# Attention and squared-ReLU layers on one core: one more batch of the first product by seven block products, with the sums moved to fit

## The chip, the cores and the metric

One core of a Trainium2 chip. The time is the device time of the kernel in microseconds (us). The kernel before takes 370.7 us: a median of 370.71 in three runs (370.69 to 371.02).

## The reference, cut to what matters

```python
# q, k, v: (8 batches, 12 heads, 448 rows, 64), fp32;  w_in: (768, 2048);  w_out: (2048, 768)
scores = (q @ k.T) / 8
attn_out = (maximum(scores, 0) ** 2 / 448) @ v        # per batch and head
x = attn_out as (8 * 448, 768)
h = x @ w_in
g = maximum(h, 0) ** 2
out = g @ w_out                                       # (3584, 768), fp32
```

## The kernel before

The kernel works in fp16 with sums in fp32. TensorE is kept busy with one long stream: h of batch 0, h of batch 1, the first O stage (`out` for the batches 0 and 1), h of batch 2, h of batch 3, the second O stage, and so on. The attention of later batches is spliced into this stream as "visits": two score tiles each time (8 matmuls), and, when a unit of four heads has all its tiles, its product with v (28 matmuls). ScalarE takes each score tile out of PSUM (where the matmuls leave their sums) with a Relu, VectorE squares it in SBUF (where the operands lie), and the product with v waits for that square.

h is made in two ways. For the batches 0 and 1 it is made directly:

```python
def h_group(b, f):                       # 16 groups f of 128 columns of w_in
    ...
        nc.tensor.matmul(cell[0][:, 0:S],                    # 6 matmuls of 448 columns
            lhsT=w1[f // 4][:, m, (f % 4) * P:(f % 4 + 1) * P],
            rhs=xts[b][:, m, :], start=(m == 0), stop=(m == NM - 1))
        ...                              # then Relu (ScalarE or VectorE), square (VectorE)
```

For the batches 2 to 7 it is made by a Strassen-like scheme: seven products of half-size blocks in place of eight. Each half of the work (`i0` 0 and 4) is 14 products of six 224-column matmuls. The scheme costs sums elsewhere: eight of w_in once (`sums_w1`), four of x for each batch (`sums_x`), and sums of products as they come out of PSUM:

```python
order = (                                # (group, product, PSUM bank, fresh bank, what follows)
    (0, 1, 0, True,  lambda: copy(0, 0, "m1", "a")),         # ScalarE: PSUM to SBUF
    (1, 1, 0, True,  lambda: copy(1, 0, "m1", "b")),
    (0, 2, 1, True,  lambda: plus(0, 1, "m1", False, False)),# VectorE: PSUM + copy, Relu, to g
    (0, 6, 0, False, lambda: copy(0, 0, "u2", "c")),         # adds into the bank just copied
    ...
    (0, 4, 0, False, lambda: relu21(0)),                     # ScalarE: Relu to g, then a square
    (1, 4, 0, False, lambda: relu21(1)),
    (0, 3, 1, False, lambda: c12(0)),                        # VectorE: sum to g, then a square
    (1, 3, 1, False, lambda: c12(1)))
```

The O stages always use such a scheme, with eight sums of w_out (`sums_w2`) made once. Before, all eight `sums_w2` and six of the eight `sums_w1` are made by VectorE during the direct h of batch 1, and the other two during the first O stage. A simple model in the kernel (`at_pe`, `at_ve`) keeps track of how far TensorE and VectorE are, and puts squares that can wait where VectorE should be free. It has no clock for ScalarE.

Of the kernel before, what the change touches and what calls it, by code (L numbers as in the profile page):

```python
# [18 lines left out]
def kernel(  # L19
# [45 lines left out]
    at_p = ctx.enter_context(tc.tile_pool(name="atp", bufs=10))  # L65
    x_p = ctx.enter_context(tc.tile_pool(name="xp", bufs=3))
    g_p = ctx.enter_context(tc.tile_pool(name="gp", bufs=1))
    early = ExitStack()
    q16_p = early.enter_context(tc.tile_pool(name="q16p", bufs=3))

# [268 lines left out]

    due: deque = deque()  # L340
    due_g: deque = deque()
    at_pe = [0.0]
    at_ve = [0.0]

# [8 lines left out]
        fn()  # L353

    def fill(until):
        for d in (due, due_g):
            while d and max(at_ve[0], at_pe[0], d[0][0]) + d[0][1] <= until:
                put(d)

# [38 lines left out]
            gts[b // 2] = g_p.tile([P, NF, 2 * S], FP16, name="g", tag="g")  # L398
        return gts[b // 2]

    def h_group(b, f):
        z = (b % 2) * S
        cell = [None]

        def step(m):
            def run():
                if m == 0:
                    cell[0] = mm_tile()
                nc.tensor.matmul(  # L409
                    cell[0][:, 0:S],  # L410
                    lhsT=w1[f // 4][:, m, (f % 4) * P:(f % 4 + 1) * P],
                    rhs=xts[b][:, m, :], start=(m == 0), stop=(m == NM - 1))
                if m < NM - 1:
                    return
                f0 = f - f % 2
                g = g_of(b)[:, f0:f0 + 2, z:z + S]
                if b == 0 and (f % 2 == 1 or f == 0) and f < 14:
                    nc.vector.tensor_scalar(
                        out=g[:, f % 2], in0=cell[0][:, 0:S],
                        scalar1=0.0, scalar2=None, op0=ALU.max)  # L420
                else:
                    nc.scalar.activation(
                        out=g[:, f % 2], in_=cell[0][:, 0:S], func=AF.Relu)
                flush()
                if b == 0 and f == NF - 1:
                    square(g)
                elif f % 2 == 1:
                    nc.vector.tensor_mul(g, g, g)
            return run

        return [(0.1892, step(m), m == 0) for m in range(NM)]
# [26 lines left out]
    def h_period(b, i0, extra):  # L458

        z = (b % 2) * S  # L460
        XY = [[None, None], [None, None]]
        keep: dict = {}

        def gs(s, hi, right=None):
            f = i0 + 2 * s + (8 if hi else 0)
            c = (slice(z, z + S) if right is None
                 else slice(z + Q, z + S) if right else slice(z, z + Q))
            return g_of(b)[:, f:f + 2, c]

        def acc(s, y):  # L470
            return XY[s][y][:, 0:S].rearrange("p (r c) -> p r c", r=2)

        def copy(s, y, nm, tag):
            t = late["m"].tile([P, S], FP32, name=nm, tag=tag)
            nc.scalar.activation(out=t, in_=XY[s][y][:, 0:S], func=AF.Copy)
            keep[s, nm] = t.rearrange("p (r c) -> p r c", r=2)

        def plus(s, y, nm, hi, right):

            now_ve(0.54)  # L480
            nc.vector._custom_dve(  # L481
                TENSOR_ADD_SAT, out=gs(s, hi, right), in0=acc(s, y),
                in1=keep[s, nm], s0=3.4e38, s1=0.0)

        def rest(g, lag):
            due_g.append((at_pe[0] + lag, 0.54,
                          lambda: nc.vector.tensor_mul(g, g, g), b))

        def relu21(s):
            nc.scalar.activation(out=gs(s, True, False), in_=acc(s, 0), func=AF.Relu)  # L490
            rest(gs(s, True), 0.8)

        def c12(s):
            plus(s, 1, "u2", False, True)
            rest(gs(s, False), 0.0)

        def left(k, f, m):

            c, n = f // 4, slice((f % 4) * P, (f % 4 + 1) * P)
            if k in (1, 2):  # L500
                return w1[c][:, m + NH * (k - 1), n]
            if k in (4, 7):
                return w1[c + 2][:, m + (NH if k == 4 else 0), n]
            return wsum[{5: 0, 6: 1, 3: 2}[k], c][:, m, n]

        def right(k, m):
            if k in (1, 2):
                return xts[b][:, m + NH * (k - 1), 0:Q]
            if k in (3, 7):
                return xts[b][:, m + (NH if k == 3 else 0), Q:S]  # L510
            return xsum[b, {5: 0, 6: 1, 4: 3}[k]][:, m]


        order = (
            (0, 1, 0, True, lambda: copy(0, 0, "m1", "a")),
            (1, 1, 0, True, lambda: copy(1, 0, "m1", "b")),
            (0, 2, 1, True, lambda: plus(0, 1, "m1", False, False)),
            (0, 6, 0, False, lambda: copy(0, 0, "u2", "c")),
            (1, 6, 0, False, lambda: copy(1, 0, "u2", "d")),
            (1, 2, 1, True, lambda: plus(1, 1, "m1", False, False)),  # L520
            (0, 5, 1, True, lambda: copy(0, 1, "m5", "a")),
            (0, 7, 0, False, lambda: plus(0, 0, "m5", True, True)),
            (1, 7, 0, False, lambda: copy(1, 0, "u3", "b")),
            (1, 5, 1, True, lambda: plus(1, 1, "u3", True, True)),
            (0, 4, 0, False, lambda: relu21(0)),
            (1, 4, 0, False, lambda: relu21(1)),
            (0, 3, 1, False, lambda: c12(0)),
            (1, 3, 1, False, lambda: c12(1)))

        FREE = {2: 0.6, 5: 0.6, 7: 0.1, 9: 0.6, 12: 0.6, 13: 1.0, 16: 0.6}  # L530

        def step(p, r, m):
            s, k, y, fresh, end = order[p]

            def run():
                if fresh and r == 0 and m == 0 and k != 5:
                    XY[s][y] = mm_tile(s)
                nc.tensor.matmul(  # L538
                    XY[s][y][:, r * Q:(r + 1) * Q],
                    lhsT=left(k, i0 + 2 * s + r, m), rhs=right(k, m),  # L540
                    start=(fresh and r == 0 and m == 0), stop=(m == NH - 1),
                    skip_group_check=not (fresh and r == 0))
                if r == 1 and m == NH - 1:
                    end()
                    for fn in extra.get(p, ()):
                        fn()
                    nx = min(n for n in FREE if n > p)
                    fill(at_pe[0] + (nx - p) * 0.576 + 0.25 + FREE[nx])
            return run



        return [(0.096, step(p, r, m), r == 0 and m == 0 and p not in (0, 1, 6, 8))
                for p in range(14) for r in range(2) for m in range(NH)]
# [8 lines left out]
                    "(p j) d -> p j d", j=J)[:, j, c],  # L563
                in_=osb[64 * i:64 * i + 64, c])

    late: dict = {}
    saved: dict = {}

    def tile_of(row):
# [289 lines left out]



    f0, f1 = h_group(0, 0), h_group(0, 1)

    def some(part):
        for _, fn, _ in part:
# [15 lines left out]
    T_H = NF * T_G  # L881
    T_S = 28 * 6 * 0.096
    T_O = [(4 if pr % 2 else 3) * 7 * KH * 0.1625 for pr in range(B // 2)]
    begin = [sum(T_O[:pr]) + 2 * (T_H + T_S * (pr - 1)) * (pr > 0) for pr in range(B // 2)]

    events = []
    seq = [[2, 3], 4, [4, 5], [6, 7], [8, 9], 5, [10, 11], [12, 13], [14, 15],
# [7 lines left out]

    def ready():
        early.close()
        for nm, n in (("s", 1), ("m", 1), ("osb", 2), ("g6", 1), ("ws", 1), ("xs", 1)):
            late[nm] = ctx.enter_context(
                tc.tile_pool(name=nm + "late", bufs=n, reuse_waits="tile"))  # L900

    events.append((T_H + 0.2, ready))
    for i in range(8):
        events.append((T_H + (1 + i // 2) * T_G, lambda i=i: sums_w2(i)))
    for i in range(6):
        events.append((T_H + (8 + i) * T_G, lambda i=i: sums_w1(i)))
    for i in range(2):
        events.append((2 * T_H + 6 + 8 * i, lambda i=i: sums_w1(6 + i)))
    for m in (6, 7):
        events.append((T_H + (1 + 3 * (m - 6)) * T_G, lambda m=m: prefetch(m)))  # L910
    at0 = T_H + 8 * T_G
    for pr in range(1, B // 2):
        t0 = 2 * NB0 * pr
        end = begin[pr] + T_S - 6.5
# [13 lines left out]
        return run  # L928

    periods: dict = {}  # L930
    for b in range(2, B):
        for i0 in (0, 4):
            extra: dict = {}
            if i0 and b % 2 == 0:
                for p, i in ((9, 0), (9, 1), (13, 2), (13, 3)):
                    extra.setdefault(p, []).append(
                        lambda b=b, i=i: sums_x(b + 1, i))
            if i0 and b % 2 == 1:
                extra[9] = [pre(b // 2, 1)]
                extra[13] = [pre(b // 2, 2)]  # L940
            periods[b, i0] = h_period(b, i0, extra)
    outs = [o_steps(pr) for pr in range(B // 2)]
    for i in (1, 2):
        events.append((2 * T_H - (3 - i) * T_G, lambda i=i: outs[0][1](i)))

    steps = [(0.1892, None, False)] * 10 + f1[4:6]
    for f in range(2, NF):
        steps += h_group(0, f)
    for f in range(NF):
        steps += h_group(1, f)  # L950
    steps += outs[0][0]
    for pr in range(1, B // 2):
        for b in (2 * pr, 2 * pr + 1):
# [6 lines left out]
    for cost, fn, edge in steps:  # L960
        fired = 0
        while ev and edge and ev[0][0] <= clock + (1.6 if edge == 2 and not fired else 1e-3):
            if len(ev[0]) == 3:
                if clock < last + 1.5:
                    break
                last = clock
            ev.popleft()[1]()
# [36 lines left out]
```

## Time and profile before

| | before |
|---|---|
| median of 3 runs | 370.71 us |
| span of the profiled run | 368.9 us, clock 0.998 |
| TensorE busy | 359.6 us (97%) |
| VectorE, ScalarE busy | 265.4 us (72%), 247.5 us (67%) |

A busy share averages stages with different limits, so the chain of work that ended last and the single stretches must be read with it. TensorE's rows in the timeline overlap (a 448-column row lasts 0.35 us, the next begins 0.19 us after it): what a stream costs is read from start to start. The view of TensorE's waits before is short; outside the first 24 us, no wait is longer than 0.3 us:

```profile
PE slot L262 <- ACT at L266: 1.4, 6, 0.3
PE mm L725 <- DVE s L594: 0.2, 1, 0.2
PE slot L317 <- DVE at L369: 0.2, 1, 0.2
```

(Who waited, for whom: us in total, number of times, the longest. "slot" at L262 are scores, at L317 the attention product with v, "mm" the products of h and `out`.)

### The profile page before, as it was taken

What the parts mean: (1) busy time and instruction counts of PE and PEld (TensorE: products, weight loads), DVE (VectorE), ACT (ScalarE), POOL (GpSimd) and SP (SyncE); (2) the same over time, 40 slices, a digit from 0 to 9 for tenths busy, and PEclk for the clock granted to TensorE, in tenths of its full rate; (3) what the DMA queues carried; (4) which work ended last, traced back from release to release, by engine and by line L of the source; (5) the groups of instructions that cost most, each with busy time, mean ns of one, the idle gap of its engine ahead of it and who ended that gap; (6) DMA issues with size and microseconds to landing.
All of it is one profiled execution on the core that took longest, in us unless ns stands there. A gap on an engine that the chain in (4) does not pass through costs nothing.

```text
span 368.9 us, 8720 instructions
## 1 busy us (share of the span) xinstructions
PE 359.6 (97%) x3588; PEld 230.3 (62%) x3588; DVE 265.4 (72%) x470; ACT 247.5 (67%) x371; POOL 107.1 (29%) x128
## 2 busy tenths in 40 slices
PE   8899999999999999999999999999999999999994
PEld 3644445445555778875555588786555689976663
DVE  2997677997777787788585766989766686884442
ACT  3988894787676989876556588886765885532220
POOL 8545521846553155531225045140000000000001
PEclk9999999999999999999999999999999999999999
DMA  8999999999999999967699899692323300003333
GB/s 115 191 207 203 205 204 162 161 158 165 190 166 127 184 101 98 115 93 62 140 166 105 159 155 86 88 116 37 65 71 88 85 3 2 2 0 85 87 92 81
DMA packets 121159, 42.64 MB, mean 116 GB/s; under 512 B 100832, under 2 KB 117760, under 8 KB 121120
## 3 DMA queue, kind: packets, MB, share of 16 engines
q0 software_dynamic: 82912, 23.01, 62.3%
q1 hardware_dynamic: 38048, 18.98, 25.7%
q8 instruction: 28, 0.46, 0.5%
q10 hardware_dynamic: 160, 0.10, 0.1%
q14 instruction: 11, 0.09, 0.1%
HBM read 45.61 MB, written 11.01 MB: 153 GB/s over the span
## 4 chain that ended last, share of the span: by engine, by line
PE 90%; ACT 3%; DVE 3%; issue 2%; DMA 1%; POOL 0%; POOLq 0%; ACTq 0%
PE mm L725 34%; PE mm L538 27%; PE slot L262 10%; PE mm L409 9%; PE slot L317 7%; ACT at L266 3%; DMA k<-in_k_dram 1%; DVE at L297 1%; PE avt L280 1%; PE slot L238 1%; PE mm L238 0%; DVE at L369 0%; DVE xt L292 0%; ACT u L627 0%; DVE osb L632 0%
## 5 line engine op out<-in xcount | busy, mean ns | idle before, releaser
L266 ACT ACTIVATE at<-slot 128x896 f16<-128x896 f32 x168 | 145.8, 925 | 22.2 <-PE slot L262 22.2
L369 DVE TENSOR_TENSOR at<-at 128x896 f16<-128x896 f16 x147 | 87.1, 617 | 9.7 <-ACT at L266 9.6
L109 POOL DMA_DIRECT2D qs<-in_q_dram x36 | 35.3, 983 | 113.7 <-DMA qT<-qs 106.2
L725 PEld LDWEIGHTS <-s 128*128 128x128 f16 x440 | 41.5, 98 | 32.7 <-issue 3.6
L262 PE MATMUL slot<-qT,kT 64*64 64x448 f16 x744 | 56.8, 361 | 1.9 <-ACT at L266 1.4
L538 PEld LDWEIGHTS <-w 128*128 128x128 f16 x576 | 54.3, 98 | 5.1 <-issue 4.3
L538 PE MATMUL mm<-xt,w 128*128 128x224 f16 x432 | 48.9, 259 | 0.0
L725 PEld LDWEIGHTS <-g 128*128 128x128 f16 x336 | 31.7, 98 | 24.1 <-issue 4.7
L538 PEld LDWEIGHTS <-ws 128*128 128x128 f16 x432 | 40.3, 98 | 4.7 <-issue 4.7
L632 DVE SCALAR_TENSOR_TENSOR osb<-mm,u 128x384 f32<-128x384 f32 (+1 forms) x30 | 16.2, 542 | 36.4 <-ACT u L627 24.0
L725 PE MATMUL mm<-b,g 128*128 128x384 f16 x224 | 40.7, 326 | 0.0
L725 PE MATMUL mm<-b,s 128*128 128x384 f16 x216 | 39.6, 326 | 0.2 <-DVE s L594 0.2
L409 PE MATMUL mm<-xt,w 128*128 128x448 f16 x192 | 39.8, 354 | 0.0
L725 PE MATMUL mm<-t,s 128*128 128x384 f16 x224 | 39.3, 326 | 0.0
L109 POOL DMA_DIRECT2D ks<-in_k_dram x36 | 35.1, 976 | 9.4 <-DMA b<-in_moe_w_out_dram 5.8
L262 PEld LDWEIGHTS <-kT 64*64 64x64 f16 x744 | 19.0, 104 | 28.7 <-issue 23.3
L561 POOL DMA_DIRECT2D out_dram<-osb x2 | 1.1, 563 | 119.6 <-DVE osb L632 119.6
L627 ACT ACTIVATE u<-mm 128x384 f32<-128x384 f32 x28 | 13.8, 492 | 31.6 <-PE mm L725 27.1
L538 PE MATMUL mm<-x,ws 128*128 128x224 f16 x288 | 34.1, 259 | 0.0
L481 DVE CUSTOM_DVE_ANT_0 g<-mm,m 128x448 f16<-128x448 f32 x36 | 22.4, 622 | 15.1 <-PE mm L538 7.3
L317 PE MATMUL slot<-at,vt 64*64 64x448 f16 x588 | 31.9, 350 | 0.2 <-DVE at L369 0.2
L409 PEld LDWEIGHTS <-w 128*128 128x128 f16 x192 | 17.1, 98 | 19.2 <-issue 5.1
(76 smaller groups left out, 399.7 us busy)
## 6 DMA issues: line engine op xcount, KB each, us to landing
out_dram<-osb SPq DMA_DIRECT2D x52, 192.0 KB, 3.0
vt<-in_v_dram POOLq DMA_DIRECT2D x24, 224.0 KB, 6.2
qs<-in_q_dram POOLq DMA_DIRECT2D x36, 112.0 KB, 4.6
ks<-in_k_dram POOLq DMA_DIRECT2D x36, 112.0 KB, 5.0
w<-in_moe_w_in_dram POOLq DMA_DIRECT2D x8, 384.0 KB, 11.9
b<-in_moe_w_out_dram POOLq DMA_DIRECT2D x4, 768.0 KB, 17.1
q<-in_q_dram POOLq DMA_DIRECT2D x6, 224.0 KB, 7.9
k<-in_k_dram POOLq DMA_DIRECT2D x6, 224.0 KB, 8.3
```

Source lines behind the costliest of these rows:

```text
L109: nc.gpsimd.dma_start(out=t[:, :, hh, :], in_=heads(src, n)[:, hh].rearrange("p (j d) -> p j d", d=D))
L238: nc.tensor.transpose(pss[i][64 * hh:64 * hh + 64, i if n < 4 else 0, j * P:(j + 1) * P], src[:, hh, j * D:(j + 1) * D], ident)
L262: nc.tensor.matmul(ps[c, hh, 0:S], lhsT=kT[r, j, c], rhs=qT[r, :, c], start=True, stop=True)
L266: nc.scalar.activation(out=at, in_=ps[:, :, 0:S], func=AF.Relu, scale=SK)
L317: nc.tensor.matmul(ps[64 * hh:64 * hh + 64, hp, 0:S], lhsT=vt[r, hh, j * D:(j + 1) * D], rhs=at[r, hh, :], start=(j == 0), stop=(j == J - 1))
L369: lambda: nc.vector.tensor_mul(at, at, at), 0))
L409: nc.tensor.matmul(cell[0][:, 0:S], lhsT=w1[f // 4][:, m, (f % 4) * P:(f % 4 + 1) * P], rhs=xts[b][:, m, :], start=(m == 0), stop=(m == NM ...
L481: nc.vector._custom_dve(TENSOR_ADD_SAT, out=gs(s, hi, right), in0=acc(s, y), in1=keep[s, nm], s0=3.4e38, s1=0.0)
L538: nc.tensor.matmul(XY[s][y][:, r * Q:(r + 1) * Q], lhsT=left(k, i0 + 2 * s + r, m), rhs=right(k, m), start=(fresh and r == 0 and m == 0), ...
L627: nc.scalar.activation(out=t, in_=X[0][:, 0:HALF], func=AF.Copy, scale=CO)
L632: nc.vector.scalar_tensor_tensor(out=osb[row][:, c], in0=acc[0][:, 0:cc.stop - cc.start], scalar=CO, in1=keep[nm][:, cc], op0=ALU.mult, op ...
L725: nc.tensor.matmul(acc[0][:, 0:HALF], lhsT=left()[:, f], rhs=right[:, f], start=(fresh and f == 0), stop=(f == KH - 1), skip_group_check=n ...
```

## The change

h of batch 1 is made by the block products too. For that the sums of w_in must be there earlier: six of the eight go into h of batch 0, two into h of batch 1. The sums of w_out are fitted between the products of h of batch 1, six of its eight squares of g move from VectorE to ScalarE, and the visits of batch 2 begin later and follow each other more closely. The core of the diff (pools, names and unused branches are cut):

```diff
-        def rest(g, lag):
+        def square_g(g, later, lag):
+            if not later:
+                nc.scalar.activation(out=g, in_=g, func=AF.Square)
+                return
             due_g.append((at_pe[0] + lag, 0.54,
                           lambda: nc.vector.tensor_mul(g, g, g), b))
         def relu21(s):
-            rest(gs(s, True), 0.8)
+            square_g(gs(s, True), b > 1, 0.8)
         def c12(s):
-            rest(gs(s, False), 0.0)
+            square_g(gs(s, False), b > 1 or i0, 0.0)
 ...
-    for i in range(8):
-        events.append((T_H + (1 + i // 2) * T_G, lambda i=i: sums_w2(i)))
     for i in range(6):
-        events.append((T_H + (8 + i) * T_G, lambda i=i: sums_w1(i)))
+        events.append(((5, 7, 8, 10, 11, 13)[i] * T_G,
+                       lambda i=i: sums_w1((0, 2, 4, 1, 3, 5)[i])))
+    events.append((15 * T_G, lambda: sums_x(1, 0)))
+    events.append((T_H, lambda: sums_w1(6)))
+    for i in (0, 1, 4, 5, 2, 3, 6, 7):
+        due_w.append((27.5 if i > 5 else 24.0, 0.87, lambda i=i: sums_w2(i), 0))
+    for t, left in ((-4.5, 6), (-2.5, 4), (0.0, 2), (1.3, 0)):
+        events.append((T_1 + t, lambda left=left: some_w(left)))
-    at0 = T_H + 8 * T_G
+    at0 = T_H + 0.75 * T_S
 ...
-    for f in range(NF):
-        steps += h_group(1, f)
+    for i0 in (0, 4):
+        steps += periods[1, i0]
 ...
-                if clock < last + 1.5:
+                if clock < last + 1.25:
```

More of the change, by code (lines that the diff above doesn't have):

```diff
@@ L67 @@
     g_p = ctx.enter_context(tc.tile_pool(name="gp", bufs=1))
+    late = {nm: ctx.enter_context(tc.tile_pool(name=nm + "late", bufs=1, side="right"))
+            for nm in ("ws", "xs", "m")}
     early = ExitStack()
@@ L341 @@
     due_g: deque = deque()
+    due_w: deque = deque()
     at_pe = [0.0]
@@ L355, in fill @@
     def fill(until):
-        for d in (due, due_g):
+        for d in (due, due_g, due_w):
             while d and max(at_ve[0], at_pe[0], d[0][0]) + d[0][1] <= until:
@@ L399, in g_of, with h_group @@
         return gts[b // 2]
-    def h_group(b, f):
-        z = (b % 2) * S
+    def h_group(f):
         cell = [None]
@@ L411, in run @@
                     lhsT=w1[f // 4][:, m, (f % 4) * P:(f % 4 + 1) * P],
-                    rhs=xts[b][:, m, :], start=(m == 0), stop=(m == NM - 1))
+                    rhs=xts[0][:, m, :], start=(m == 0), stop=(m == NM - 1))
                 if m < NM - 1:
@@ L415, in run @@
                 f0 = f - f % 2
-                g = g_of(b)[:, f0:f0 + 2, z:z + S]
-                if b == 0 and (f % 2 == 1 or f == 0) and f < 14:
+                g = g_of(0)[:, f0:f0 + 2, 0:S]
+                if (f % 2 == 1 or f == 0) and f < 14:
                     nc.vector.tensor_scalar(
@@ L424, in run @@
                 flush()
-                if b == 0 and f == NF - 1:
+                if f == NF - 1:
                     square(g)
@@ L564, in store @@
                 in_=osb[64 * i:64 * i + 64, c])
-    late: dict = {}
     saved: dict = {}
@@ L858 @@
         name="mma", bufs=2, space=PSUM, reuse_waits="tile")))
-    f0, f1 = h_group(0, 0), h_group(0, 1)
+    f0, f1 = h_group(0), h_group(1)
     def some(part):
@@ L883 @@
     T_O = [(4 if pr % 2 else 3) * 7 * KH * 0.1625 for pr in range(B // 2)]
-    begin = [sum(T_O[:pr]) + 2 * (T_H + T_S * (pr - 1)) * (pr > 0) for pr in range(B // 2)]
+    begin = [sum(T_O[:pr]) + (T_H + T_S * (2 * pr - 1)) * (pr > 0) for pr in range(B // 2)]
+    T_1 = T_H + T_S
     events = []
@@ L897, in ready @@
         early.close()
-        for nm, n in (("s", 1), ("m", 1), ("osb", 2), ("g6", 1), ("ws", 1), ("xs", 1)):
+        for nm, n in (("s", 1), ("osb", 2), ("g6", 1)):
             late[nm] = ctx.enter_context(
@@ L902, with some_w @@
     events.append((T_H + 0.2, ready))
-    for i in range(8):
-        events.append((T_H + (1 + i // 2) * T_G, lambda i=i: sums_w2(i)))
     for i in range(6):
-        events.append((T_H + (8 + i) * T_G, lambda i=i: sums_w1(i)))
-    for i in range(2):
-        events.append((2 * T_H + 6 + 8 * i, lambda i=i: sums_w1(6 + i)))
+        events.append(((5, 7, 8, 10, 11, 13)[i] * T_G,
[4 more added lines that the diff above has]
+        due_w.append((27.5 if i > 5 else 24.0, 0.87, lambda i=i: sums_w2(i), 0))
+    def some_w(left):
+        while len(due_w) > left:
+            put(due_w)
+    for t, left in ((-4.5, 6), (-2.5, 4), (0.0, 2), (1.3, 0)):
+        events.append((T_1 + t, lambda left=left: some_w(left)))
     for m in (6, 7):
         events.append((T_H + (1 + 3 * (m - 6)) * T_G, lambda m=m: prefetch(m)))
-    at0 = T_H + 8 * T_G
+    at0 = T_H + 0.75 * T_S
     for pr in range(1, B // 2):
@@ L930 @@
     periods: dict = {}
-    for b in range(2, B):
+    for b in range(1, B):
         for i0 in (0, 4):
             extra: dict = {}
+            if b == 1 and i0 == 0:
+                for p, i in ((0, 1), (1, 2), (5, 3)):
+                    extra[p] = [lambda i=i: sums_x(1, i)]
+                extra[9] = [lambda: sums_w1(7)]
             if i0 and b % 2 == 0:
@@ L937 @@
                         lambda b=b, i=i: sums_x(b + 1, i))
-            if i0 and b % 2 == 1:
+            if i0 and b % 2 == 1 and b > 1:
                 extra[9] = [pre(b // 2, 1)]
@@ L943 @@
     for i in (1, 2):
-        events.append((2 * T_H - (3 - i) * T_G, lambda i=i: outs[0][1](i)))
+        events.append((T_1 - (3 - i) * 1.15, lambda i=i: outs[0][1](i)))
     steps = [(0.1892, None, False)] * 10 + f1[4:6]
     for f in range(2, NF):
-        steps += h_group(0, f)
-    for f in range(NF):
-        steps += h_group(1, f)
+        steps += h_group(f)
+    for i0 in (0, 4):
+        steps += periods[1, i0]
     steps += outs[0][0]
```

## The prediction

> **What bounds the kernel now.** I read first the busy shares of the engines, then the slices, then the chain that ended last.
>
> ```profile
> span 368.9 us, 8720 instructions
> PE 359.6 (97%) x3588; PEld 230.3 (62%) x3588; DVE 265.4 (72%) x470; ACT 247.5 (67%) x371; POOL 107.1 (29%) x128
> PE   8899999999999999999999999999999999999994
> DVE  2997677997777787788585766989766686884442
> PEclk9999999999999999999999999999999999999999
> PE 90%; ACT 3%; DVE 3%; issue 2%; DMA 1%; POOL 0%; POOLq 0%; ACTq 0%
> ```
>
> TensorE is the bound: full in every slice but the first two and the last, at full clock, and 90% of the chain that ended last is its own matmuls. There is no slack behind it, so a product taken away is worth its whole time, and a new wait of TensorE costs its whole time too. VectorE is at 72% on average, but the average hides the stretch that the change touches. The table of busy time by stretch, for h of batch 0 and then h of batch 1:
>
> ```profile
> 24.00:56.60 32.60, 32.04 (x343) 14.47 (x336) 23.67 (x43) 26.95 (x36) 14.42 (x17) 1.00 1.28 204
> 56.60:78.70 22.10, 22.10 (x146) 10.34 (x146) 20.20 (x29) 15.83 (x26) 10.57 (x12) 1.00 1.85 157
> ```
>
> (Columns: stretch, length, busy PE, PEld, DVE, ACT, POOL.) In the second row TensorE is busy 22.10 of 22.10 us and VectorE already 20.20: it makes the sums of both weights there. In the first, VectorE is busy 23.67 of 32.60 and ScalarE 26.95.
>
> The rates, from the chain in order of time and from the timeline of VectorE:
>
> ```profile
> 56.65 10.32 PE mm L409 x54
> 305.48 21.96 PE mm L538 x228
> 59.05 1.82 DVE L152 TENSOR_TENSOR t<-b,b 128x1536 f16<-128x1536 f16 x2
> 46.63 1.15 DVE L369 TENSOR_TENSOR at<-at 128x896 f16<-128x896 f16 x2
> 49.08 2.66 ACT L266 ACTIVATE at<-slot 128x896 f16<-128x896 f32 x3
> ```
>
> A 448-column matmul costs 10.32/54 = 0.191 us in a stream, a 224-column one 21.96/228 = 0.0963. A single row's duration (0.35 and 0.26) has the pipeline's depth in it and is not used. One VectorE instruction overlaps the next by about 0.07 us: 0.87 us a weight sum, 0.54 a square, 0.54 a sum that reads PSUM, 0.42 a sum of x, 0.60 a sum of g. ScalarE takes some 0.83 us for 896 columns and 0.45 for 448 in a row, and 0.92 and 0.54 until the result is there.
>
> **What the Trainium skill says.** "TensorE: Matmul & The Clock Gate", Part 2, step 3: throughput is one column of the moving operand per cycle, so halving columns halves a matmul. The trace agrees: 0.0963 against 0.191. "VectorE: DVE Perf Modes", the perf-mode tier table: tensor_tensor reaches at most 2x on 16-bit operands in SBUF and 1x with PSUM. The trace agrees: a 128x896 square out of SBUF and a 128x448 sum with PSUM both take 0.62. So nothing on VectorE gets cheaper by being moved. "ScalarE: Activation LUTs", step-by-step: one element per cycle and lane whatever the function, so a Square of 128x896 should cost what a Relu of that size costs, some 0.83 us in a row; that is an estimate, as no ScalarE square is in this trace. It is dearer than the same square on VectorE (0.54).
>
> **The change part by part.**
>
> Removed: 96 matmuls of 448 columns, 96 x 0.191 = 18.35 us. Added: 28 products of 6 matmuls of 224 columns, 168 x 0.0963 = 16.18 us. Gain on the bounding engine **2.17 us**. By the order of the two programs all other matmuls are the same in number, and the streams are broken by scores 86 times in both.
>
> Added to VectorE: 12 sums from PSUM (6.5 us) and four sums of x (1.7), less eight squares of g on 896 columns, of which six go to ScalarE and two stay late (4.3 - 1.1 = 3.2): +5 us, in a stretch two us shorter that had 2 us free. Therefore six of the eight sums of w_in (6 x 0.87 = 5.2 us) move into h of batch 0, and two of them come in from the O stage. ScalarE gets 12 copies and 6 squares for its 16 Relus. All this is beside TensorE only where it is in time. I walked the new orders with the durations above and found three places where it is not.
>
> (a) In h of batch 0 the fourth sum of w_in stands straight ahead of the squares of visit 12, 13. Before, these were made at 46.63 to 47.78, and the attention product that reads the second of them reaches it at about 47.86 (start 46.72, 24 of 28 matmuls at 0.047). With 0.87 us ahead of it the square ends at 48.65: TensorE waits **0.8 us**. The sixth sum is ahead of the squares for the last attention product; 0.47 us of idle time is there to take it and the rest, some **0.3 us**, is waited for (before, TensorE already waited for that square at 56.27). The first, second, third and fifth fall in gaps of 1 to 2 us and cost nothing. Their weights landed: the last was issued at 28.86 and takes 12 us.
>
> (b) Between the two halves of h of batch 1 ScalarE has in a row Relu, Square, Relu, three Squares, and then the copy of the first product of the second half. Call T the start of h of batch 1. Product 11 starts at T + 5.9 and its Relu 0.78 later at T + 6.6 (as in the trace, matmul start to consumer). Then Relu 0.54 + 0.06, Square 0.83, Relu 0.60, three Squares 2.5, copy 0.54: T + 11.7. The fourth product of the second half adds into the bank which that copy reads, and TensorE comes to it at 0.1 + 17 x 0.576 = T + 9.9. It waits about **1.7 us**.
>
> (c) From the eighth product of the second half on, VectorE has without a gap: four sums from PSUM 2.2, seven squares of scores 3.8, two of g 1.1, the last four sums of w_out 3.5, s1 and s2 1.2, one output sum 0.5, so 12.3 us up to the last square for the attention product inside the first O group. TensorE needs about 10.8 us to get there: seven products 4.0, three pairs of scores 1.7, two O products 2.6, another pair 0.6, an O product and half a pair 1.6, most of the attention product. The wait is some **1 to 2 us**; ScalarE, late with its Squares, holds up the scores' buffers and the first O copy in the same place. I put 1.7.
>
> Sum: -2.17 + 0.8 + 0.3 + 1.7 + 1.7 = +2.3 us, which makes 373.0. The visits of batch 2 begin some 3 us later and closer together (one per 1.95 instead of 2.19 us of the schedule's clock); they use gaps that VectorE (28.4 of 40.1 us busy) and ScalarE (28.0) have in the first O stage, and move no total. Transfers stay as they are.
>
> **The rivals.**
>
> *Everything stays hidden.* Then only TensorE's work counts: 370.7 - 2.2 = 368.5. For it: VectorE was already at 20.2 of 22.1 without TensorE losing time, and the change has evidently been fitted by a schedule that tracks VectorE's time. Against it: the edge at 47.8 and the row of ScalarE in (b), which that schedule does not track.
>
> *Half of it.* (a) and part of (b) are real, and (c) is taken up because squares can be made earlier than I put them: stalls of 1.5 to 2.5, 370 to 371.
>
> *VectorE becomes the bound for longer.* If the backlog of (c) is carried through the first O stage with its closer visits, each attention product waits again: 2 us more, 375. Against it: VectorE has 12 us to spare in that stage, even after three more visits.
>
> *Transfers.* Closer visits ask for q, k and v of a unit every 7 us or so instead of 8. Against a wait there: they are asked for two units ahead, the median from issue to landing is about 5 us for a load and 4.3 for a transpose.
>
> **Range and chances.** The walk gives 373.0; the first two rivals together have perhaps two chances in five, because a change so carefully placed was probably tried out. I settle at **372.4 us**. The gain can't be more than 2.17, and the stalls I see add to 4.5 at most about 6.5, so the range is **369.6 to 374.8**. Faster by 2% would need 7.4 us (chance 0.01); slower by 2% the same the other way (0.03); within 2% 0.96.
>
> **What would show it.** In the profile after: the h products of batch 1 as 168 more rows of the 128x224 form, TensorE's busy time some 2 us lower. For (a), TensorE waiting in the timeline at 47.7 to 48.7 for a square of scores. For (b), a gap of TensorE 10 us after h of batch 1 starts, released by a ScalarE copy of a product, with Squares of 0.9 us ahead of it. For (c), the attention product of the first O group waiting for VectorE. If TensorE has none of these, the time is 368.5 and the walk was wrong in the durations; if waits stand in later stages, the moved visits did it.

## The result, and the profile after

| | before | after |
|---|---|---|
| median | 370.70 us (370.58 to 371.02, 4 runs) | 374.39 us (374.10 to 374.75, 4 runs) |
| ratio after to before | | 1.0099 (95% interval 1.0081 to 1.0116) |
| span of the profiled run | 368.9 us | 372.5 us, clock 0.999 |
| waits of TensorE over 0.3 us after the first 24 us | none | 4 |

The change costs 3.7 us, where 1.7 had been forecast. That is within 2%, as forecast, and clear of the noise: the interval leaves out 1. Run a second time, it was 374.44 beside 371.04.

The busy times and the engines of the chain, after:

```profile
PE 359.8 (97%) x3660; PEld 237.9 (64%) x3660; DVE 270.9 (73%) x480; ACT 252.9 (68%) x377; POOL 107.3 (29%) x128
PE 85%; DVE 7%; ACT 4%; issue 1%; DMA 1%; POOLq 0%; POOL 0%; ACTq 0%
```

The chain that ended last has 5 points less of TensorE and 4 more of VectorE in it: it now leaves TensorE. TensorE's busy time has not fallen by 2 us, as I had expected it to. A part of each stop counts as busy in this row (the stop in (b) below is 1.84 us from start to start and 1.69 as a wait), so it does not show a gain that comes with stops; in e5 below, which has none of them, it is 358.3. TensorE's waits tell more:

```profile
PE slot L264 <- ACT at L268: 1.9, 7, 0.4
PE mm L544 <- ACT m L478: 1.7, 1, 1.7
PE slot L319 <- DVE at L372: 1.4, 6, 0.3
```

One wait of 1.7 us for a ScalarE copy (b in the prediction) and six waits of the attention product for VectorE's squares (a and c). I take them in order of time. For (a), the timeline of VectorE in h of batch 0, after, then that of TensorE beside it, its first line before and the others after:

```profile
46.13 0.62 DVE L431 TENSOR_TENSOR g<-g 128x896 f16<-128x896 f16 x1
46.67 0.95 DVE L181 TENSOR_TENSOR ws<-w 128x1536 f16<-128x1536 f16 x1
47.54 1.15 DVE L372 TENSOR_TENSOR at<-at 128x896 f16<-128x896 f16 x2
```

```profile
46.72 1.49 PE L317 MATMUL slot<-at,vt 64*64 64x448 f16 x28
46.76 1.12 PE L319 MATMUL slot<-at,vt 64*64 64x448 f16 x20
48.21 0.38 PE L319 MATMUL slot<-at,vt 64*64 64x448 f16 x4 [0.33 <-DVE at L372]
48.74 0.38 PE L319 MATMUL slot<-at,vt 64*64 64x448 f16 x4 [0.15 <-DVE at L372]
```

The squares began at 46.63 before; now a sum of w_in is ahead of them and they begin at 47.54. The 28 matmuls of the attention product, in one piece before, come in three. By starts, the two stops cost 0.84 us; with the second place of the same kind (0.31 us more than before, at 57.5) h of batch 1 starts at 58.95 instead of 57.72, that is 1.2 us late.

For (b), the timeline around the two halves of h of batch 1, after:

```profile
65.47 0.55 ACT L496 ACTIVATE g<-mm 128x448 f16<-128x448 f32 x1 [0.60 <-PE mm L544]
66.05 0.95 ACT L490 ACTIVATE g<-g 128x896 f16<-128x896 f16 x1
66.90 0.53 ACT L496 ACTIVATE g<-mm 128x448 f16<-128x448 f32 x1
67.00 1.89 PE L544 MATMUL mm<-xt,w 128*128 128x224 f16 x18
67.46 2.63 ACT L490 ACTIVATE g<-g 128x896 f16<-128x896 f16 x3
70.00 0.96 ACT L478 ACTIVATE m<-mm 128x448 f32<-128x448 f32 x2
70.57 1.31 PE L544 MATMUL mm<-x,ws 128*128 128x224 f16 x12 [1.69 <-ACT m L478]
```

Relu, Square, Relu, three Squares, and only then the copies (L478). TensorE had finished its first three products of the second half and could not add into the bank that the copy still had to read. It starts 11.6 us after h of batch 1 does; I had worked out 11.7.

For (c), VectorE and the attention product at the start of the first O stage, after:

```profile
82.23 1.82 DVE L154 TENSOR_TENSOR nt<-b,t 128x1536 f16<-128x1536 f16 x2
83.97 0.55 DVE L637 SCALAR_TENSOR_TENSOR osb<-mm,m 128x384 f32<-128x384 f32 x1
84.40 0.95 PE L319 MATMUL slot<-at,vt 64*64 64x448 f16 x16
84.44 0.62 DVE L493 TENSOR_TENSOR g<-g 128x896 f16<-128x896 f16 x1
84.97 2.23 DVE L372 TENSOR_TENSOR at<-at 128x896 f16<-128x896 f16 x4
85.64 0.38 PE L319 MATMUL slot<-at,vt 64*64 64x448 f16 x4 [0.29 <-DVE at L372]
```

The product begins at 84.40, and VectorE begins the row of squares of which it needs the first three at 84.97, after the last sums of w_out, an output sum and a square of g. There is no gap on VectorE. By starts this product loses 1.2 us. The scores before the first O stage, at 78.36 to 79.48, waited 0.42 us for a buffer behind ScalarE's Squares; without these Squares (e9 below) that stage starts 0.77 us earlier. So (c) is 1.9 us in all.

### The profile page after: what moved, and what is told of

Same layout as the page of the kernel before. It is cut to its first block, busy times and chain, and to the rows that moved or that the text cites. A ratio compares the mean times of both kernels' runs of the same rounds, so it can differ in the third digit from the quotient of the medians.

```text
span 372.5 us, 8886 instructions
## 1 busy us (share of the span) xinstructions
PE 359.8 (97%) x3660; PEld 237.9 (64%) x3660; DVE 270.9 (73%) x480; ACT 252.9 (68%) x377; POOL 107.3 (29%) x128
## 4 chain that ended last, share of the span: by engine, by line
PE 85%; DVE 7%; ACT 4%; issue 1%; DMA 1%; POOLq 0%; POOL 0%; ACTq 0%
PE mm L730 33%; PE mm L544 30%; PE slot L264 10%; PE slot L319 7%; PE mm L412 4%; ACT at L268 2%; DVE at L372 2%; DMA q<-in_q_dram 1%; DVE at L299 1%; ACT g L490 1%; PE avt L282 1%; PE slot L240 1%; PE mm L240 0%; DVE g L421 0%; DVE nt L154 0%
## 5 line engine op out<-in xcount | busy, mean ns | idle before, releaser
L544 PEld LDWEIGHTS <-w 128*128 128x128 f16 x672 | 63.4, 98 | 5.8 <-issue 4.9
L264 PE MATMUL slot<-qT,kT 64*64 64x448 f16 x744 | 57.5, 361 | 2.4 <-ACT at L268 1.9
L544 PE MATMUL mm<-xt,w 128*128 128x224 f16 x504 | 56.8, 259 | 0.0
L544 PEld LDWEIGHTS <-ws 128*128 128x128 f16 x504 | 47.3, 98 | 6.4 <-issue 6.4
L544 PE MATMUL mm<-x,ws 128*128 128x224 f16 x336 | 39.6, 259 | 1.7 <-ACT m L478 1.7
L484 DVE CUSTOM_DVE_ANT_0 g<-mm,m 128x448 f16<-128x448 f32 x42 | 26.2, 623 | 19.7 <-PE mm L544 10.6
L319 PE MATMUL slot<-at,vt 64*64 64x448 f16 x588 | 32.7, 350 | 1.4 <-DVE at L372 1.4
L478 ACT ACTIVATE m<-mm 128x448 f32<-128x448 f32 x42 | 22.6, 549 | 13.3 <-PE mm L544 10.8
L484 DVE CUSTOM_DVE_ANT_0 g<-mm,u 128x448 f16<-128x448 f32 x42 | 25.8, 620 | 7.1 <-ACT xt L325 2.9
```

The source lines that it names most:

```text
L264: nc.tensor.matmul(ps[c, hh, 0:S], lhsT=kT[r, j, c], rhs=qT[r, :, c], start=True, stop=True)
L319: nc.tensor.matmul(ps[64 * hh:64 * hh + 64, hp, 0:S], lhsT=vt[r, hh, j * D:(j + 1) * D], rhs=at[r, hh, :], start=(j == 0), stop=(j == J - 1))
L478: nc.scalar.activation(out=t, in_=XY[s][y][:, 0:S], func=AF.Copy)
L484: nc.vector._custom_dve(TENSOR_ADD_SAT, out=gs(s, hi, right), in0=acc(s, y), in1=keep[s, nm], s0=3.4e38, s1=0.0)
L544: nc.tensor.matmul(XY[s][y][:, r * Q:(r + 1) * Q], lhsT=left(k, i0 + 2 * s + r, m), rhs=right(k, m), start=(fresh and r == 0 and m == 0), ...
```

## The experiments

All were run in five rounds beside the kernel before. "Over before" is the difference of the medians. The changed kernel itself is 3.7 and 3.4 over before in its two series, so a difference of less than 0.3 us between two experiments says nothing by the times alone. The traces tell finer differences: counted from the first h of batch 0 (up to there the runs differ by some tenths), the stream of TensorE in e10 keeps within 0.01 us of that of the first trace of the same kernel all the way. "By the trace" means this count.

| run | result | median, us | before beside it | over before | ratio |
|---|---|---|---|---|---|
| e1_wsums_moved | correct | 373.08 | 370.73 | +2.35 | 1.0056 |
| e2_no_four_squares | wrong | 372.23 | 370.73 | +1.50 | 1.0033 |
| e3_visits_later | correct | 374.93 | 370.73 | +4.20 | 1.0105 |
| e4_less_wout_sums | wrong | 373.06 | 370.73 | +2.33 | 1.0058 |
| e5_waits_taken_out | wrong | 369.23 | 371.00 | -1.77 | 0.9952 |
| e6_before_w_in_early | correct | 372.34 | 371.00 | +1.34 | 1.0032 |
| e7_refitted | correct | 369.89 | 371.00 | -1.11 | 0.9969 |
| e8_refitted_again | wrong by mistake | 370.22 | 371.04 | -0.82 | 0.9981 |
| e9_no_last_two_squares | wrong | 374.08 | 371.04 | +3.04 | 1.0085 |
| e10_changed_again | correct | 374.44 | 371.04 | +3.40 | 1.0093 |

The theory: three places where a part of the change stands ahead of something that TensorE needs, each a loss of its own, adding up. The main rival: VectorE and ScalarE are simply full in this stretch, and a wait taken away at one place comes back at another.

**e1_wsums_moved.** The fourth and sixth sums of w_in behind the squares.

```diff
-        events.append(((5, 7, 8, 10, 11, 13)[i] * T_G,
+        events.append(((5, 7, 8, 11, 11, 15)[i] * T_G,
```

> The changed kernel, with two of the six sums of w_in in h of batch 0 moved: the fourth behind the squares of visit 12, 13 and the sixth behind the square of visit 20. Same instructions, same number. Theory (three separate waits of TensorE add up to the loss): the waits for squares at 48.2 to 48.7 us and at 57.5 us of the changed kernel's trace vanish, h of batch 1 starts about 1.2 us earlier (57.75 instead of 58.95), and the whole is 1.2 us faster: 373.2. Rival (the lost time is one backlog of VectorE that is only passed on): the sixth sum now lies in h of batch 1, its waits grow by what the earlier ones shrink, and the whole stays within 0.4 us of 374.4.

2.35 over before instead of 3.4 to 3.7, so 1.1 to 1.3 us were won by order alone. The five timed runs lie between 372.85 and 373.46; only the profiled run was slow (413 us at a clock of 0.851), so its trace is not compared. The rival falls for this place: in the traces of e5 and e7, which have the same edit and are fast, h of batch 1 starts 1.17 us earlier, and the sum that was pushed into it takes nothing of that back.

**e6_before_w_in_early.** The same question from the other side: the kernel before, plus only the early sums of w_in.

```diff
-        events.append((T_H + (8 + i) * T_G, lambda i=i: sums_w1(i)))
+        events.append(((5, 7, 8, 10, 11, 13)[i] * T_G,
+                       lambda i=i: sums_w1((0, 2, 4, 1, 3, 5)[i])))
```

> The kernel before, h of batch 1 direct as ever, with only one part of the change: the six sums of w_in made in h of batch 0 at the changed kernel's places. Theory: the same squares come late, TensorE waits 0.8 us and 0.4 us in h of batch 0, nothing gives this back though VectorE has 5 us less to do in h of batch 1, and the whole is 1.2 us slower: 371.9. Rival (VectorE's relief afterwards gives it back, or the sums were harmless without the other parts): within 0.3 us of 370.7.

1.34 over before; by the trace 1.19 at the end of the first O stage. Its timeline has the stops of the changed kernel, to the digit:

```profile
47.06 1.12 PE L318 MATMUL slot<-at,vt 64*64 64x448 f16 x20
48.51 0.38 PE L318 MATMUL slot<-at,vt 64*64 64x448 f16 x4 [0.33 <-DVE at L370]
49.05 0.38 PE L318 MATMUL slot<-at,vt 64*64 64x448 f16 x4 [0.15 <-DVE at L370]
```

VectorE has 5 us less to do afterwards, and nothing of the loss comes back: by the trace it is still 1.19 us at 290. TensorE was full already.

**e2_no_four_squares.** Without ScalarE's four Squares between the halves.

```diff
             if not later:
-                nc.scalar.activation(out=g, in_=g, func=AF.Square)
+                if i0:
+                    nc.scalar.activation(out=g, in_=g, func=AF.Square)
                 return
```

> The changed kernel without the four Squares that ScalarE makes at the end of the first half of h of batch 1 (wrong result on purpose: those columns of g stay unsquared). Theory: the copy that the fourth product of the second half waits for comes some 3 us earlier, the wait of 1.7 us vanishes, and the whole is 1.7 to 1.9 us faster: 372.6. Rival (VectorE would have been the next to hold the same product up, by its sums from PSUM and its sums of w_out): the wait moves to VectorE and less than 0.7 us is won.

1.50 over before, 1.9 to 2.2 us better than the changed kernel, and TensorE's wait for a copy is gone from the profile; nothing takes its place. In the trace the last product of the last group of the second O stage starts at 206.66 instead of 208.58; 0.08 of that lies before the first h of batch 0, so 1.84 us is the better figure, which is the stop of (b) from start to start.

**e4_less_wout_sums.** Without the last three sums of w_out.

```diff
+        if op == 3 or i == 3:
+            return
 ...
-            (X, False, lambda: tile_of(rows[1])[:, HI], nt4, end4),
+            (X, False, lambda: tile_of(rows[1])[:, HI], b21, end4),
```

> The changed kernel without the last three sums of w_out (one half of one, both of another: 2.6 us of VectorE; wrong result on purpose, the products take unsummed blocks). Theory: VectorE's backlog in front of the attention product of the first O group is 2.6 us shorter, its waits (1.2 us in three pieces) vanish, the 0.65 us behind ScalarE's Squares stay, and the whole is 1.1 us faster: 373.3. Rival (ScalarE's lateness alone delays those squares): less than 0.4 us is won.

2.33 over before, 1.1 to 1.4 us better; by the trace 1.17. The attention product of the first O stage no longer waits; the 0.42 us of the scores stay. VectorE's backlog causes the larger part of (c).

**e9_no_last_two_squares.** Without ScalarE's two Squares in the second half.

```diff
-                nc.scalar.activation(out=g, in_=g, func=AF.Square)
+                if not i0:
+                    nc.scalar.activation(out=g, in_=g, func=AF.Square)
```

> The changed kernel without the two squares that ScalarE makes in the second half of h of batch 1 (wrong result on purpose); the four of the first half stay. Theory: the wait of scores for their buffer (0.4 to 0.65 us at 79.2 us of the changed kernel's trace) comes from these squares and goes, the attention product's wait for VectorE's squares stays or shrinks a little: 0.5 to 0.9 us faster than the changed kernel run beside it. Rival (VectorE's backlog alone sets the start of the O stage, so what is won before it is lost in front of the attention product): less than 0.2 us.

This one went against my theory. The scores' wait is gone, but the first of the three stops of the attention product grows from 0.29 to 0.94 us. The row of TensorE's waits in total:

```profile
PE slot L319 <- DVE at L372: 1.8, 4, 0.9
```

By the trace the O stage starts 0.77 us earlier, and 0.12 is left of it after the attention product; the medians say 0.36, which is at the limit of what they can tell. So ScalarE's lateness lay in front of VectorE's backlog and was mostly hidden by it. (c) is one loss of 1.9 us with two causes that overlap: VectorE's backlog alone makes 1.8 of it (this run), ScalarE's Squares alone 0.8 (e4).

**e3_visits_later.** The first visits of batch 2 after h of batch 1.

```diff
-    at0 = T_H + 0.75 * T_S
+    at0 = T_H + T_S + 3.5
```

> The changed kernel with the visits of batch 2 begun 7.4 us later by the schedule's clock, so that none lies in h of batch 1 and the first attention product comes in the second O group; they then lie closer together (one per 1.6 us of that clock instead of 1.95). Theory: the waits at the start of the first O stage (0.65 us of score buffers behind ScalarE, 1.2 us of the attention product behind VectorE's squares) vanish and the whole is 1 to 1.9 us faster, 372.5 to 373.4. Rival (VectorE and ScalarE are short over h of batch 1 and the first O stage together): the waits turn up later in that stage, in the closer visits, and the whole stays within 0.5 us or gets slower.

4.20 over before: 0.5 to 0.8 us worse. The rival was right here. The attention product did come later and the waits of (c) went, but then an O product waits 0.8 us for an output sum on VectorE, and the second attention product of the now closer visits waits 0.5 us for squares:

```profile
PE mm L544 <- ACT m L478: 1.7, 1, 1.7
PE slot L319 <- DVE at L372: 1.4, 5, 0.4
PE mm L730 <- DVE osb L637: 0.8, 1, 0.8
```

By the trace the run is 0.15 us behind the changed kernel after the first O stage and 0.41 at the end. Moving all the visits moves the wait. Taking the one right thing out of VectorE's queue, as in e4, does not.

**e5_waits_taken_out.** The edits of e1 and e4, and all six ScalarE Squares left out.

> The changed kernel with the three edits at once: the two sums of w_in moved, the squares that ScalarE makes in h of batch 1 left out (all six this time), the last three sums of w_out left out (wrong result on purpose). Theory: the three losses are separate and add: 1.3 for the sums of w_in, 2.15 for the first four squares, 0.6 more for the other two, 1.3 for the sums of w_out, 5.35 us together, so 369.0, and what is left under the kernel before is the bare gain of the block products, about 2 us less a few tenths of closer visits. Rival (the losses overlap, one wait hides behind another): 370 or more. If it came out well under 368.5, the gain would be larger than 28 products at 0.576 us against 16 groups at 1.135 allow.

1.77 under before. From 3.4 to 3.7 over, that is 5.2 to 5.5 us, and the single edits add to 1.2 + 2.05 + 1.2 + 0.36 = 4.8 (middle values). By the trace it is 4.97 us against 1.17 + 1.84 + 1.17 + 0.12 = 4.30. (a), (b) and (c) add; inside (c) the two causes overlap, and what is left over here is the 0.65 us that e9 won at the scores and lost again at the attention product. None of the waits of (a), (b) and (c) is left. By the trace the stream is 1.84 us ahead of the kernel before after the first O stage, of the 2.0 that the products are worth, and 1.55 at the end.

**e7_refitted.** The same work, correct, in other places.

```diff
-        events.append(((5, 7, 8, 10, 11, 13)[i] * T_G,
+        events.append(((5, 7, 8, 11, 11, 15)[i] * T_G,
 ...      # of the six ScalarE Squares the first stays, the others are kept:
+                    due_s.append(fn)
 ...      # one behind the second, one behind the fifth product of the second half
+                extra[1] = [lambda: due_s.popleft()()]
+                extra[4] = [lambda: due_s.popleft()()]
 ...      # three Squares and the last two sums of w_out in the first O group
+    events.append((T_1 + 5.0, lambda: sums_w2(6)))
+    events.append((T_1 + 5.0, lambda: sums_w2(7)))
+    for t in (3.8, 5.0, 5.8):
+        events.append((T_1 + t, lambda: due_s.popleft()()))
```

> A version meant to be correct and better: the changed kernel with the two sums of w_in moved; of the six ScalarE squares only the first stays at its place, the second and third go behind copies of the second half, three into the first O group; the last sums of w_out go behind the squares that the first attention product there waits for. No instruction is added or dropped. Theory (only the places were wrong, not the amount of work): most of the 5.3 us of waits goes and the time is 369.2 to 370.2, below the kernel before. Rival (VectorE and ScalarE are full in that stretch, so that a wait taken away at one place turns up at another): 371.5 or more.

369.89 us, correct, 1.11 under before and 4.5 to 4.8 us under the changed kernel, with the same instructions in the same numbers. Its busy row:

```profile
PE 358.9 (97%) x3660; PEld 238.1 (65%) x3660; DVE 270.6 (73%) x480; ACT 252.4 (69%) x377; POOL 107.1 (29%) x128
```

VectorE and ScalarE are as busy as in the changed kernel (270.9 and 252.9). They were not too full in this stretch as a whole; their queues were in the wrong order. This is the best version found: it beats both kernels, the one before by 0.3% (95% interval of the ratio 0.9957 to 0.9982).

**e8_refitted_again.** The late Squares further apart, at 3.8, 5.8 and 7.0.

> The refitted version, with the last two of its three late ScalarE squares further apart in the first O group. In its profile one wait of TensorE is left in that stage, 0.4 us for a buffer of scores behind two squares in a row. Theory: that wait goes, 0.3 to 0.5 us faster than the first refit, 369.5. Rival (a square anywhere in that stage delays the next scores as much): no change, 369.9.

A miss, in two ways. The result is wrong by a mistake of mine: the sum of g rows for the second group is made with that group's first product, which the schedule puts at 6.5, ahead of the square at 7.0, so that the sum read columns that were not yet squared. And the wait of 0.4 us for a score buffer behind ScalarE went from one pair of scores to the next pair (0.26) and to the attention product after it (0.42). By the trace 0.4 us was lost against e7.

**e10_changed_again.** The changed kernel, unedited.

> The changed kernel itself once more, beside the others, so that they can be compared on one chip: 374.4 again, 1.0099 times the kernel before, whatever the theory.

374.44 us, 1.0093 times before, with the waits of its first trace at the same places. The result stands.

## Why the prediction was wrong, point by point

The direction and the mechanism, three stops of TensorE behind work put ahead of what it needs, were right; their sizes were too small, the visits were left out, and 0.6 us was taken off without a reading. The loss was forecast at 1.7 us and is 3.7. The median lies inside the range that was given, near its upper end.

- **What bounds the kernel.** Right. TensorE's stops were each paid in full, and e6 shows that one of 1.2 us is not given back.
- **(a), "0.8" and "some 0.3".** 0.84 and 0.31 by the trace, 1.1 to 1.3 together by e1 and 1.34 by e6. Right.
- **(b), "about 1.7 us".** 1.69 us of wait for the copy, 1.84 from start to start and by e2's trace. Right, slightly small. The Square's cost in it, "some 0.83 us in a row", was called an estimate and holds: one Square took 0.95 and three in a row 2.63, so 0.84 for each further one. The Trainium skill, "ScalarE: Activation LUTs", What ACT_TABLE_LOAD costs, has 186 ns + 0.833 ns per element for one with immediate scale and bias, less 93 ns between neighbours: by estimate 0.93 and 0.84 us for 896 columns.
- **(c), "I put 1.7".** 1.9 by the trace (0.77 before the O stage, 1.17 in the attention product). The place and both engines were right, and so was VectorE's row, 12.3 us (74.36 to 86.66). That the wait comes so near is in part luck. The row begins 0.9 us after the eighth product does (73.47), which the walk left out, and TensorE's way was put too short: 10.8 us, where the terms listed add to 10.5 before the attention product and to 11.6 with "most" of it (24 matmuls at 0.047), and e5, without a stop, takes 11.3. So 13.2 less 11.3 was read as 12.3 less 10.8.
- **"Removed: 96 matmuls of 448 columns, 96 x 0.191 = 18.35 us".** A little too large. The 10.32 us that I divided by 54 end with a break of 0.1 us before the next scores. From start to start a 448-column matmul takes 0.189 us and a 224-column one 0.096, which makes the gain 18.15 - 16.13 = 2.0 instead of 2.17.
- **"They use gaps ... and move no total".** This step failed. The closer visits have a cost in the first O stage. The lines of the chain that ended last, after, for three pairs of scores and two attention products there:

```profile
91.90 0.67 PE slot L264 x8
98.51 0.61 PE slot L264 x8
103.74 0.61 PE slot L264 x8
106.08 1.44 PE slot L319 x28
115.87 1.52 PE slot L319 x28
```

Such a pair takes 0.50 and such a product 1.32 wherever nothing is in its way, so these five rows lose 0.7 us. Before, one attention product of this stage lost 0.44 (1.76 us from its start to that of the scores behind it):

```profile
113.97 1.43 PE L317 MATMUL slot<-at,vt 64*64 64x448 f16 x24
115.55 0.38 PE L317 MATMUL slot<-at,vt 64*64 64x448 f16 x4 [0.15 <-DVE at L369]
```

That makes 0.2 to 0.3 us more than before, where I had put nothing; e5, with no other stop left in the stretch, is 0.2 short of the full gain there. Capacity was there, as I had said, but not at those moments.
- **"I settle at 372.4 us".** This is the other step that failed, and the one that put 1.7 us where the walk had 2.3. The walk gave 373.0, and I took 0.6 off because "a change so carefully placed was probably tried out". That is no reading of the profile. The places that I had checked were right to a quarter of a microsecond, and nothing in the trace spoke for the rivals' lower times.

Together, in us, from the walk's +2.3: 0.15 for the gain, 0.2 for (a) and (b), 0.24 for (c), and 0.2 to 0.3 for the visits make +3.1 to +3.2. By the trace TensorE's stream is 3.13 behind after the first O stage. It is 3.25 behind after h of the batches 2 and 3 and 3.42 from the third O stage on; the spans say 3.5. So 0.3 us is lost in later stages. e5 and e7 lose at least as much there, so it does not come from (a), (b) or (c); which part of the change makes it was not tested and stays open.

Of the rivals, "everything stays hidden" (368.5) is what e5 comes near to when every cause is cut out, and what e7 approaches by order alone. "Half of it" did not happen: none of the three stops was taken up. "VectorE becomes the bound for longer" did not happen in the changed kernel, and did in part in e3. For "Transfers" there is no sign: no wait of TensorE after the first 24 us is for a transfer.

## What to carry to other kernels

Where one engine is full, a piece of work on another engine can cost nothing or almost its whole length (here 0.84 us for one sum of 0.87, and nothing for the first three), and which of the two is decided by what stands behind it in that engine's queue, not by the engine's share of busy time. Two late engines in front of one stop need not add: in (c), 1.8 us of the one and 0.8 of the other made 1.9. Before moving work into "free" time, walk the queue at that place with measured durations: what is next, when does the full engine need it, and how many hundredths of a microsecond were left. A schedule model that tracks one helper engine will load the other one blindly: here the row of Squares on ScalarE, which had no clock in the model, was the dearest single wait. And when such a walk has been done, do not take its figure back on a guess: here 2.3 us were walked, 1.7 forecast and 3.7 measured.

## What the Trainium skill lacked or had wrong

- "TensorE: Matmul & The Clock Gate", Back-to-back issue gap: it gives 131 ns per matmul of 512 columns as the sustained rate of weight load and matmul pairs, and calls its formula N/2.4 + 2.5 ns too high for large N. In this case each matmul has its own weight load, and the streams run at 189 ns for 448 columns and 96 ns for 224: what the formula gives (189 and 96), so the sustained rate of the page does not hold for these streams. No run here has 512 columns.
- "Perfetto Trace Analysis", Optimizing Scalar/DVE Operations: it says that moving some work to ScalarE may make sense if VectorE is saturated. What it lacks there is a look at what the moved work then stands in front of: four Squares so moved held up a copy of 0.5 us behind them, and TensorE for 1.7 us.
